# A decode kernel of two interleaved layers: the load of ScalarE's function table first on its engine, and new orders of the same tasks on four engines

## The chip, the cores and the metric

The kernel runs on one core of a Trainium2 chip. The core has five instruction streams that run side by side and meet through semaphores: TensorE (PE in the profile, its weight loads PEld), VectorE (DVE), ScalarE (ACT), GpSimd (POOL) and SyncE (SP), which here does nothing but issue transfers. Each engine works through its instructions strictly in the order in which they are written; an instruction whose semaphore has not come yet holds up everything behind it on that engine. The metric is the device time of one launch in microseconds (us), as the median of several runs. Times inside the kernel come from the profile of one further execution.

## What is computed

Eight batches, each with one row of D = 448 numbers, go through an attention layer (A) and an MLP layer (B), and then through both once more with the same weights and the same K and V caches:

```python
def _A_ref(x, k_cache, v_cache, wq, wo):          # Hq = 16, Hkv = 8, Dh = 256
    W = min(4096, max(256, Sk // 4))              # Sk = 4096, W = 1024
    q = (x @ wq)                                  # 448 x 4096, 16 heads of 256
    k = jnp.repeat(k_cache[:, :, Sk - W:, :], 2, axis=1)
    v = jnp.repeat(v_cache[:, :, Sk - W:, :], 2, axis=1)
    p = _softmax(einsum("bhqd,bhkd->bhqk", q, k) * Dh ** -0.5)
    return einsum("bhqk,bhkd->bhqd", p, v) @ wo   # 4096 x 448

def _B_ref(x, w1, w2):                            # F = 1792
    return _silu(x @ w1) @ w2

x = A_x
x = x + _A_ref(_layernorm(x), ...)
x = x + _B_ref(_layernorm(x), ...)
x = x + _A_ref(_layernorm(x), ...)
x = x + _B_ref(_layernorm(x), ...)
```

All is bf16. Only the last W = 1024 positions of each cache are read: per batch eight K heads and eight V heads of 1024 x 256, 512 KB each.

## The kernel before

**Data.** One K or V head fills one of R = 30 slots in SBUF, `slots`, 128 partitions by 2048 numbers. `load_kv` (L453, its DMA at L456) loads them in the sequence batch 0 K0 to K7, V0 to V7, batch 1 K0 to K7 and so on; a slot is loaded again once its last reader is done. wq, wo, w1 and w2 are loaded once: wq ahead of the first K, wo and w2 behind batch 0's K7, w1 behind its V7. The last two slots, 28 and 29, serve as scratch space at the start (x, the squares, the first q, the row sums of wo and w2, and the place into which ACT writes what it only wants to sum); the loads that take them over wait for those uses. Both layers read a head out of the same slot, so the second attention of a batch must run while its K and V are still there.

**Stages.** Each batch b runs through these, named by the strings that the code gives to its tasks:

- *start*, once for all batches (`start_rows`, L569): constants are cleared on DVE (L330 to L377, bank clears at L350 and L352 of the eight PSUM banks among them); x is turned into columns on PE ("xT", into bank 7), masked on DVE ("xb0", L576), its statistics are made ("sq8" on ACT, L547; "sqh8", "st8" on DVE; "stat8" on PE), it is centred ("x0", DVE), multiplied by wq for all batches at once ("q1", L591), and brought into the form that the scores need ("q1r", "q1T", "q1sel", and "q1s", one half copied by DVE, the other by ACT).
- *row sums* (`row_sums`, L426), once: the mean of each row of wo and w2 is written beside it, so that the layer norm's mean comes out of the same product. Groups of rows take turns between DVE ("rsum2", "rsum3", L435; the copy "rsumd", L438) and ACT ("rsum", L443, twenty of them; the copy "rsumd", L447).
- *layer 1 attention*: POOL spreads q over the key heads in two halves ("qbd1", L622); DVE transposes each K slot in two halves ("KT0" to "KT7", L632); PE makes the scores in eight blocks, four for K0 to K3 and four for K4 to K7 ("S0.0", "S0.1", L648); softmax (L657): DVE maximum and its spreading ("max0" L665 to "mb0" L669), ACT exp (L672), PE permutation ("perm0", L674), DVE transposition ("turn0", L676), sums of the rows (L680) and their reciprocals. Then the values in two parts ("PVA" L729 for V0 to V3, "PVD" L748 for V4 to V7); each part is copied out by ACT ("oevA.0", "oevA.1" L715; "oevD" L723), turned by PE ("oTA", "oTD", L702) and scaled by DVE ("oTevA", "oTevD", L696). The output projection runs in two halves ("woA", "woD", L801) and is copied out by ACT ("rowb1", L1091).
- *chain* (L856): residual and layer norm ("xinit", "fold1", the x column "xb1" L827, "stat1" L834, ACT's variance "var1" L837, POOL's power "pow1" L839), the MLP ("w1" L518, its turn "yT" L538, "tanh" L846, "hT" L847, "w2" L865, "rowb2" L869), the next residual and norm ("fold2", "xb2", "x2b", "stat2", "var2", "pow2"), and q of layer 2 in two halves ("wq0", "wq1" L892; "qT" L538, "qm" L901, "qd" L905, and ACT's copy "qbd2" L909).
- *layer 2 attention* of the same batch ("S1.0", "S1.1", "max1", "exp1", ..., values "PV1.0", "PV1.1", L729, "oev1" L723), interleaved with layer 1 of the next batch.
- *tail*: batches 0 to 6 are taken together through layer 2's output projection and MLP beside batch 7's chain (`final_rows`, L912: "wo8", "w18", "tanh8" L978, "h8" L979, "w28" L983, "rowb9" L991); batch 7 ends by itself (`final_last`, L997).

PE also gets short fillers: `busy` (L850) puts in products with zeros ("zero", L853, 48 of them) whose results nobody reads.

**What sets the order.** The code above does not fix the order in which an engine runs its tasks. `Plan.add` (L56) only records each task with the tiles that it reads and writes. `schedule` (L91) then lays out each of the four computing engines by a string in `ORDER` (L16 to L35): every character is a base-62 digit, the place of the next task among those of this engine that are left, in program order ("0" is the first one left; "." announces two digits). PE has 509 tasks, DVE 421, ACT 167, POOL 38. SP is not in the table: its loads stay in program order. `emit` (L108) then works out which semaphores each task must wait for, so that the same data flows whatever the order; ACT issues its three transfers ahead of its tasks.

The load of ACT's function table is one such task:

```python
act(lambda e: e.preload_act_table_set("exp_and_others"), [], [], -1, "init")     # L328
```

It reads and writes no tile, so nothing waits for it and it may stand anywhere on ACT. In the order of before it is ACT's 73rd task, behind the exp of batch 3.

Of the kernel before, what the change touches and what calls it, by code (L numbers as in the profile page):

```python
# [14 lines left out]

ORDER = {  # L16
    "pe": (
        "0000000q11111111133311c11312221130000033001700510330011117777000400444433200011610440333022021000220"
        "1777101000111117777000030444433200011615551002201101000220006051000111111777700040044443320001166151"
        "4002201120103300006605100011111777700040044442220001161551400220110100330000605103001111177770004004"  # L20
        "4443220001161551400220110100333990010000011111177770004004444232000111551400220111010002200066055100"
        "cccc0000006000044444320001107066605504401220000c22aaa22801050002014403355550222333355553322523432201"
        "000111000"),
    "dve": (
        "2AB1liliiv4vousks2uquCuxAoO15xxJxd8s5vIpsBt4ooxb6clojllftvjfcnmm82g9f0h8d3e6bdc9a3435114402110082302"
        "54202210098880870705ab0abc0088700555550000000a08980870705aa09a09097700555550000000098880870605ab09a0"
        "b097700555550000000a08989078005ab09a0b087700555550000100a08889078005aa09a0b097700555550000000a089890"
        "77060baa09c0087700555550000100a089807770d0b5aa0ab9901005555500001100acia0g90e8a098706004440300100022"
        "011333312122211110000"),
    "act": (  # L30
        "12222233232222322c22a3333632221111111113312112111111111331211111111111130201000000000000220100000000"
        "0000220110000000000022010000000000030201110100000403300001111101010"),
    "pool": (
        "00000011001102200301032002200201001000"),
}  # L35


# [1123 lines left out]
```

## Time and profile before

| | |
|---|---|
| time, median of 3 runs | 233.13 us (232.94, 233.13, 233.14) |
| time of the profiled execution | 235.56 us |
| its span, first to last instruction | 233.7 us |
| mean granted clock of TensorE | 0.963 |
| busy: PE | 170.5 us, 73% of the span, 3616 matmuls |
| busy: PE's weight loads | 93.5 us, 40% (beside the matmuls) |
| busy: DVE | 158.4 us, 68%, 421 instructions |
| busy: ACT | 68.2 us, 29%, 203 instructions |
| busy: POOL | 22.8 us, 10%, 42 instructions |
| moved by DMA | 78.20 MB |

How to read what follows. A row of the timeline has the time of its start from the start of the span, its length, its engine, its line in the kernel, the operation, output and input tiles with their shape, how many instructions it sums up, and in brackets the idle time of the engine just before it with what ended it. The chain of waits is the sequence of work that ended last, followed back from the last instruction. A row of the windows gives, for one stretch of time, the busy time of each engine and its number of instructions. The granted clock is the share of full speed that TensorE was given. Tiles are named by their allocation: a name such as slot or w_sb stands for all buffers of that name, and qbd holds, beside q, the exponentials and the probabilities.

### The profile page before, as it was taken

To read this page: it belongs to the slowest core of one execution; us is meant where nothing else is said; L and a number is where in the kernel's file an instruction comes from. 1 tells how busy PE (TensorE), PEld (TensorE's weight loads), DVE (VectorE), ACT (ScalarE), POOL (GpSimd) and SP (SyncE) were. 2 spreads that over 40 slices of the span, in tenths; PEclk is the share of its full clock that TensorE was granted. 3 is DMA by queue.
4 is the path that set the end of the run, shared out by engine and by line. 5 is a ranking of instruction groups with operands and counts; after the bars stand their busy time and mean duration, and the time that the engine had idled before them with its cause. 6 is when DMAs were issued, how large, how long until landed. Compare 5 with 4: busy or idle time off the path is not lost.

```text
span 233.7 us, 8172 instructions
## 1 busy us (share of the span) xinstructions
PE 170.5 (73%) x3616; PEld 93.5 (40%) x3616; DVE 158.4 (68%) x421; ACT 68.2 (29%) x203; POOL 22.8 (10%) x42
## 2 busy tenths in 40 slices
PE   0000562368879887988898898879797978899985
PEld 0000530123444454445444443544363335556453
DVE  6029998967874995588488649947675597355642
ACT  2000003995223323321532233233213322143321
POOL 1000220001200200200021011002000110010200
PEclk9999999559999999999999999999799999999999
DMA  6999999999999999999999999999999999500000
GB/s 165 411 407 409 380 380 396 412 407 410 403 405 405 407 409 364 410 408 405 391 407 409 360 365 416 408 403 407 407 365 263 414 407 363 191 3 3 3 4 4
DMA packets 23401, 78.20 MB, mean 335 GB/s; under 512 B 3127, under 2 KB 6086, under 8 KB 22982
## 3 DMA queue, kind: packets, MB, share of 16 engines
q1 hardware_dynamic: 22806, 77.30, 85.2%
q8 instruction: 28, 0.46, 0.8%
q10 hardware_dynamic: 560, 0.38, 0.7%
q14 instruction: 7, 0.06, 0.1%
HBM read 77.67 MB, written 0.01 MB: 332 GB/s over the span
## 4 chain that ended last, share of the span: by engine, by line
PE 43%; SPq 21%; DMA 14%; DVE 10%; ACT 6%; issue 4%; POOL 1%; DVEq 0%; ACTq 0%
DMA slot<-in_A_k_cache_dram 14%; SPq L456 12%; PE bank L648 10%; PE bank L729 6%; SPq L413 6%; DVE slot L632 4%; PE bank L892 3%; PE bank L801 3%; PE bank L518 3%; PE bank L865 2%; PE bank L748 2%; PE bank L853 2%; PE bank L905 2%; PE bank L702 2%; PE bank L674 1%
## 5 line engine op out<-in xcount | busy, mean ns | idle before, releaser
L632 DVE STREAM_TRANSPOSE slot<-slot 128x512 uint32<-128x512 uint32 x128 | 82.7, 686 | 19.2 <-DMA slot<-in_A_k_cache_dram 19.0
L648 PE MATMUL bank<-slot,qbd 128*16 128x256 bf16 (+1 forms) x1024 | 40.8, 287 | 6.8 <-ACT qbd L909 3.3
L729 PE MATMUL bank<-slot,qbd 128*4 128x512 bf16 (+1 forms) x384 | 28.6, 388 | 7.2 <-DVE w_sb L438 6.2
L648 PEld LDWEIGHTS bank<-slot,qbd 128*16 128x16 bf16 (+1 forms) x1024 | 23.2, 88 | 18.2 <-ACT qbd L909 6.5
L839 POOL TENSOR_TENSOR fcols<-fcols 128x1 f32<-128x1 f32 x17 | 9.4, 554 | 117.8 <-ACT fcols L837 107.5
L672 ACT ACTIVATE qbd<-bank,mm 128x256 bf16<-128x256 f32 x17 | 8.0, 472 | 36.9 <-DVE mm L669 36.9
L676 DVE STREAM_TRANSPOSE qbd<-bank 128x256 bf16<-128x256 bf16 x17 | 8.1, 478 | 15.0 <-PE bank L674 15.0
L892 PE MATMUL bank<-wq_sb,xbz 128*2 128x256 bf16 x512 | 17.2, 275 | 0.1
L853 PE MATMUL bank<-ident,cols 128*128 128x512 bf16 x48 | 16.7, 403 | 0.0
L622 POOL TENSOR_TENSOR qbd<-q1s,fcols 128x256 bf16<-128x256 bf16 x16 | 9.6, 614 | 63.5 <-PE bank L702 58.1
L801 PE MATMUL bank<-wo_sb,q1s 128*1 128x449 bf16 x252 | 15.5, 368 | 0.1
L729 PEld LDWEIGHTS bank<-slot,qbd 128*4 128x4 bf16 (+1 forms) x384 | 7.9, 84 | 17.9 <-DVE w_sb L438 6.4
L909 ACT ACTIVATE qbd<-bank 128x256 bf16<-128x256 f32 x16 | 6.1, 383 | 30.1 <-PE bank L905 30.1
L715 ACT ACTIVATE qbd<-bank 128x256 bf16<-128x256 f32 x20 | 7.7, 383 | 18.6 <-PE bank L729 16.2
L892 PEld LDWEIGHTS bank<-wq_sb,xbz 128*2 128x2 bf16 x512 | 11.3, 82 | 3.8 <-DVE xbz L827 1.7
L538 DVE STREAM_TRANSPOSE bank<-bank 128x256 f32<-128x256 f32 (+1 forms) x25 | 10.8, 436 | 2.9 <-PE bank L518 1.7
L748 PE MATMUL bank<-slot,qbd 128*12 128x512 bf16 (+3 forms) x124 | 11.2, 410 | 1.3 <-ACT qbd L715 1.3
L723 ACT ACTIVATE qbd<-bank 128x512 bf16<-128x512 f32 x14 | 8.3, 594 | 12.5 <-PE bank L748 10.3
L865 PE MATMUL bank<-w_sb,q1s 128*1 128x449 bf16 x98 | 7.2, 382 | 5.5 <-DVE q1s L847 5.5
L665 DVE TENSOR_REDUCE mm<-bank 128x1 f32<-128x256 f32 x17 | 7.2, 421 | 5.6 <-PE bank L648 5.1
L696 DVE TENSOR_TENSOR q1s<-bank,q1s 128x16 bf16<-128x16 f32 (+1 forms) x18 | 3.0, 167 | 10.3 <-PE bank L702 9.8
L551 PE MATMUL bank<-xb,cols 128*128 128x8 bf16 x4 | 0.3, 172 | 13.1 <-DVE slot L549 13.1
(164 smaller groups left out, 231.4 us busy)
## 6 DMA issues: line engine op xcount, KB each, us to landing
slot<-in_A_k_cache_dram SPq DMA_DIRECT2D x64, 512.0 KB, 8.6
slot<-in_A_v_cache_dram SPq DMA_DIRECT2D x64, 512.0 KB, 11.1
wo_sb<-in_A_wo_dram SPq DMA_DIRECT2D x1, 3584.0 KB, 25.7
wq_sb<-in_A_wq_dram SPq DMA_DIRECT2D x3, 1024.0 KB, 8.6
w_sb<-in_B_w_dram SPq DMA_DIRECT2D x1, 1568.0 KB, 28.1
w_sb<-in_B_w_dram SPq DMA_DIRECT2D x1, 1344.0 KB, 17.5
wq_sb<-in_A_wq_dram SPq DMA_DIRECT2D x1, 256.0 KB, 3.5
wq_sb<-in_A_wq_dram ACTq DMA_DIRECT2D x1, 256.0 KB, 4.0
```

The costliest lines, as they stand in the source:

```text
L413: dma(lambda e: e.dma_start(w2_sb[:].rearrange("p (g n) -> p g n", n=PW)[:, :, R0:M1], B_w2.rearrange("(g p s) n -> p g (s n)", p=P, s=2)) ...
L456: dma(lambda e: e.dma_start(slots[s][:, :].rearrange("p (u d) -> p u d", d=DH), cache[b, kvh, S0:SK, :].rearrange("(p u) d -> p u d", p=P) ...
L538: dve(lambda e: e.transpose(view(bank[bi][:], n, [(2, n // 32), (n // 16, 16), (1, 2)]), bank[bi][:, 0:n].rearrange("p (g r s) -> p g r s" ...
L622: pool(lambda e, k2=k2: e.tensor_tensor(qdata(0, k2), q1s[:, b, 64 * k2:64 * k2 + 64].rearrange("p (n r) -> p n r", r=2).unsqueeze(3) .bro ...
L632: dve(lambda e, v=v: e.transpose(v, v), SL(s, h), SL(s, h), b, "KT%d" % k)
L648: fns.append(lambda e, w=w, j=j, kv=kv, cb=cb, par=par: e.matmul(sc[32 * j:32 * j + up_to, 0:256], w, kv, start=(cb == 0 and par == 0), st ...
L729: return [lambda e, u=u: e.matmul(bank[OB[L] if ob is None else ob][32 * j:32 * j + 2 * n, :], pT_sb[L if qi is None else qi][:, pcol(u, c ...
L748: pe([lambda e, t=t, c0=c0, w=w, kvh=kvh: e.matmul(bank[OB[0]][32 * t:32 * t + 2 * w, :], pT_sb[0][:, pcol(2 * t, c0):pcol(2 * t, c0) + 2 ...
L801: fns.append(lambda e, i=i, w=w, c0=c0: e.matmul(bank[XB][32 * (i % 4):32 * (i % 4) + 1, c0:c0 + D + 1], oT(i), w, start=(i < 4), stop=(i ...
L853: pe(lambda e: e.matmul(bank[SC[1]][:, :], cols[:, 3:4].broadcast_to([P, P]), view(ident[:], 0, [(0, 4), (1, P)]), start=True, stop=True), ...
L865: fns.append(lambda e, f=f, w=w, c0=c0: e.matmul(bank[XB][32 * (f % 4):32 * (f % 4) + 1, c0:c0 + D + 1], hTr[b][:, f:f + 1], w, start=(f < 4),
L892: pe([lambda e, j=j, c=c, s=s, wb=wb, k2=k2: e.matmul(bank[wb][32 * j:32 * j + 2, 0:256], pair(b, xcol(c, k2), s), view(wq_sb[:], c * HD + ...
```

## The change

Only the four strings of `ORDER` change. The tasks, what each reads and writes, the loads, and SP's order are the same; so are all sizes.

```diff
 ORDER = {
     "pe": (
-        "0000000q11111111133311c11312221130000033001700510330011117777000400444433200011610440333022021000220"
-        "1777101000111117777000030444433200011615551002201101000220006051000111111777700040044443320001166151"
...
+        "00v00000111111111333121b1333310410005500390277222010111117777000002444420210901105003330201100003300"
+        "1700500300111117777000030444442200011615551002201100003302006055000201111777700003044444220001115144"
...
     "dve": (
-        "2AB1liliiv4vousks2uquCuxAoO15xxJxd8s5vIpsBt4ooxb6clojllftvjfcnmm82g9f0h8d3e6bdc9a3435114402110082302"
...
+        "qGoQIji1z.161kwIv.111iuttEx3kBSBBPra95Exxx80qgxlIC6rpppxfkcmvh4cbis1qp25i6ha2gce51abam424f7402444847"
...
     "act": (
-        "12222233232222322c22a3333632221111111113312112111111111331211111111111130201000000000000220100000000"
-        "0000220110000000000022010000000000030201110100000403300001111101010"),
+        "00222231233334f4413b44422252220110000000201100000000000022011000000000002201100000000000220110000000"
+        "0000220110000000000022011000000000030201110100000403300001100001010"),
     "pool": (
-        "00000011001102200301032002200201001000"),
+        "00010301001000100200020000100201001000"),
 }
```

Read back into tasks, the strings say this:

- **ACT.** The table load is the first task. At the start, before ran sq8, exp0 of batch 0, and then the row sums; after, five row sums stand between sq8 and that exp. Two of ACT's copies of row sums come later: w2's first behind oevA.0, w2's second behind var1 of batch 0. In the last batch rowb9 comes ahead of the evacuation oevL0.0; smaller swaps between neighbouring batches are left out here.
- **DVE.** At the start, before clears five banks and some constants first, masks x at place 22 and transposes the first K half (slot 0) at place 27. After, three banks (6, 1, 0) and six small constants come first, the 10th task is the first half of slot 1, the clear of bank 7 is the 12th, the mask of x again the 22nd; K0 is transposed 69th and 71st. Of the sixteen K halves of batch 0 fifteen stand ahead of q's "q1T" and all ahead of "q1s", where before ten and eleven did; rsum3 and one rsum2 stand ahead of max0 of batch 0. In the later batches oTevD comes ahead of the next batch's KT0, four K halves stand between it and xb1, and in batches 3 to 5 three halves instead of two between xb1 and yT. In the last batch h8 comes behind the second maximum.
- **PE.** The first filler stands ahead of q1; in batch 0 the second q1sel is earlier, woA stands behind oTD, and no filler is left between fold1, stat1 and w1. The four blocks of S1.1 stand three ahead of perm0 and one behind it in most turns (all four ahead in batch 0, one in batch 5), where they were two and two in most. From batch 3 on woA stands behind oTD, and one PV1.1 ahead of oTD. stat2 stands ahead of wq0 in batches 0 to 5, where before it did so in batch 5 alone. Fillers move: batch 4 has none between w1 and w2 (before, batch 5 had none there). In the last batch the first of the two permutations and xinitL stand ahead of w28.
- **POOL.** The two halves of qbd1 of batch 0 change places; pow1 and pow2 stand ahead of the second qbd1 half in several batches.

More of the change, by code (lines that the diff above doesn't have):

```diff
@@ L17 @@
     "pe": (
-        "0000000q11111111133311c11312221130000033001700510330011117777000400444433200011610440333022021000220"
-        "1777101000111117777000030444433200011615551002201101000220006051000111111777700040044443320001166151"
-        "4002201120103300006605100011111777700040044442220001161551400220110100330000605103001111177770004004"
-        "4443220001161551400220110100333990010000011111177770004004444232000111551400220111010002200066055100"
-        "cccc0000006000044444320001107066605504401220000c22aaa22801050002014403355550222333355553322523432201"
@@ L23 @@
-        "000111000"),
-    "dve": (
-        "2AB1liliiv4vousks2uquCuxAoO15xxJxd8s5vIpsBt4ooxb6clojllftvjfcnmm82g9f0h8d3e6bdc9a3435114402110082302"
[L26 to L29, printed above, removed]
+        "00v00000111111111333121b1333310410005500390277222010111117777000002444420210901105003330201100003300"
@@ new lines @@
+        "1700500300111117777000030444442200011615551002201100003302006055000201111777700003044444220001115144"
+        "4410011101103300177166111101111777700003044444320001161144441001110110022280166111101111177770000304"
+        "4443320001161144441001110100330017771111101111177770050004444422000116114444100111011033a09207710100"
+        "cccc000000600004444322100110706660550440122000022bbb22980105000201440335555j302233335555332242232015"
+        "100011100"),
+    "dve": (
+        "qGoQIji1z.161kwIv.111iuttEx3kBSBBPra95Exxx80qgxlIC6rpppxfkcmvh4cbis1qp25i6ha2gce51abam424f7402444847"
+        "5663344413bb0aa11981816c0a0a9a0088700555504000000098980870605bb0aba0077700555550000000088880870605bb"
+        "0a9a0077700555550000000098880877060bba0ba0077700555550000000098880877005bb0a9a0087700555550000000098"
+        "880778060bba099007770055555000000090888807870b0aac099990100555550000110b0cib09g90d080777050444030200"
+        "0022224033311122211110000"),
```

## The prediction

> **What bounds the kernel now.** I read the page first, then the windows, the chain of work that ended last, and the timeline. From the page: the span, the granted clock in 40 slices of 5.84 us, and the K transposes on DVE (count, then busy and mean ns, then idle before).
>
> ```profile
> span 233.7 us, 8172 instructions
> PEclk9999999559999999999999999999799999999999
> L632 DVE STREAM_TRANSPOSE slot<-slot 128x512 uint32<-128x512 uint32 x128 | 82.7, 686 | 19.2 <-DMA slot<-in_A_k_cache_dram 19.0
> ```
>
> From the windows (stretch, its length, then busy us of PE, PEld, DVE, ACT, POOL, the granted clock, DMA share and GB/s):
>
> ```profile
> 0.00:15.30 15.30, 0.36 (x5) 0.28 (x5) 4.02 (x26) 1.51 (x2) 0.70 (x6) 1.00 0.88 316
> 15.30:36.05 20.75, 8.85 (x221) 6.36 (x221) 18.00 (x61) 0.00 (x0) 2.85 (x3) 1.00 1.04 391
> ...
> 160.00:170.00 10.00, 8.45 (x141) 3.96 (x129) 7.26 (x17) 2.75 (x8) 1.74 (x3) 0.83 1.03 408
> ```
>
> The DMA engines stream at about 400 GB/s all through: at 408 a 512 KB slot (524,288 bytes) takes 1.28 us. Transposing a K slot takes two DVE instructions of 82.7/128 = 0.65 us. Now the chain (start, length, what):
>
> ```profile
> 47.50 15.63 DMA slot<-in_A_k_cache_dram
> ...
> 67.55 0.44 DVE mm L665
> ...
> 88.85 0.44 DVE mm L665
> ...
> 152.81 0.44 DVE mm L665
> ...
> 179.29 9.99 DMA slot<-in_A_k_cache_dram
> ...
> 195.07 1.08 PE bank L648 x32
> ```
>
> And one row of the timeline, the first maximum of batch 6:
>
> ```profile
> 175.57 0.42 DVE L665 TENSOR_REDUCE mm<-bank 128x1 f32<-128x256 f32 x1 [0.57 <-PE bank L648]
> ```
>
> Up to 63 us the chain is loading. Then each batch takes one turn from its first softmax maximum (L665) to the next: 88.85 - 67.55 = 21.30 us, and (152.81 - 67.55)/4 = 21.32 on average. Sixteen slots want 16 x 1.28 = 20.5 us of DMA, less than a turn, so the turn is bound by the handshakes of PE, ACT, DVE and POOL. The turn up to 175.57 took 22.76: its granted clock is the 0.83 above. At the end the last K loads come back into the chain (179.29), and from 195 us the last batch runs out on PE.
>
> **The change, part by part.** *The table load.* From ACT's timeline:
>
> ```profile
> 2.57 1.28 ACT L547 ACT_TABLE_LOAD   x1 [2.57 <-issue]
> 5.26 0.23 ACT L547 ACTIVATE slot<-xb 128x32 f32<-128x32 bf16 x1 [1.40 <-DVE xb L576]
> ...
> 111.89 1.28 ACT L328 ACT_TABLE_LOAD   x1
> ...
> 113.96 0.38 ACT L715 ACTIVATE qbd<-bank 128x256 bf16<-128x256 f32 x1 [0.79 <-PE bank L729]
> ```
>
> Before has two loads. One stands at 2.57, put before the first activation because L328's own is far down the order; it is behind ACT's three DMA issues and ends at 3.85. L328's own is at 111.89, in batch 3. With L328 first I expect one load, again behind those DMA issues and over long before ACT is needed. The one at 111.89 ends at 113.17 and its engine then waits 0.79 us more for PE, so taking it away gives 0.0 (bounds 0 and, if its cover were gone, -1.28). The Trainium skill ("ScalarE: Activation LUTs", What ACT_TABLE_LOAD costs) speaks of about 2.66 us for a switch, a drain included. By that ACT would have been held until about 114.5, past the 113.96 at which it started: this trace shows 1.28 and no drain. A load into the set already active may differ; I leave it as a rival.
>
> *The start.* Rows of the timeline, in order of time:
>
> ```profile
> 1.25 2.65 DVE L331 MEMSET bank<- 128x512 f32 x5
> 15.32 0.71 DVE L632 STREAM_TRANSPOSE slot<-slot 128x512 uint32<-128x512 uint32 x1 [9.58 <-DMA slot<-in_A_k_cache_dram]
> 36.05 0.42 DVE L665 TENSOR_REDUCE mm<-bank 128x1 f32<-128x256 f32 x1 [0.71 <-PE bank L648]
> 37.23 2.91 DVE L435 TENSOR_REDUCE slot<-wo_sb 128x6 f32<-128x2688 bf16 x1
> 37.41 0.47 ACT L672 ACTIVATE qbd<-bank,mm 128x256 bf16<-128x256 f32 x1 [31.92 <-DVE mm L669]
> 39.24 0.58 ACT L443 ACTIVATE slot<-w_sb 128x448 bf16<-128x448 bf16 x1 [1.27 <-DMA w_sb<-in_B_w_dram]
> 39.94 0.58 ACT L443 ACTIVATE slot<-w_sb 128x448 bf16<-128x448 bf16 x1
> 40.06 3.93 DVE L435 TENSOR_REDUCE slot<-w_sb 128x4 f32<-128x1792 bf16 x2
> 53.91 0.22 ACT L447 ACTIVATE wo_sb<-slot 128x6 bf16<-128x6 f32 x1
> 54.22 2.58 DVE L632 STREAM_TRANSPOSE slot<-slot 128x512 uint32<-128x512 uint32 x4 [0.62 <-DMA slot<-in_A_k_cache_dram]
> 54.28 0.93 PE L801 MATMUL bank<-wo_sb,q1s 128*1 128x449 bf16 x16
> 55.27 0.55 ACT L1091 ACTIVATE rowb<-bank 128x450 bf16<-128x450 f32 x1 [0.47 <-PE bank L801]
> 63.16 0.71 DVE L632 STREAM_TRANSPOSE slot<-slot 128x512 uint32<-128x512 uint32 x1 [0.41 <-DMA slot<-in_A_k_cache_dram]
> 63.80 0.42 DVE L538 STREAM_TRANSPOSE bank<-bank 128x256 f32<-128x256 f32 x1
> 65.47 2.04 PE L648 MATMUL bank<-slot,qbd 128*16 128x256 bf16 x64 [0.47 <-ACT qbd L909]
> ```
>
> Before, DVE clears its constants first (4.02 us of work), then stands 9.58 us at slot 0 of K. After, the tenth DVE task is the transpose of slot 1, which lands one slot later: 15.3 + 1.3 = 16.6. Behind it stand the clear of bank 7, on which PE's first transposition of x waits, and so the whole path to q; and most of the clears. What stands ahead of it is three bank clears (3 x 0.53) and six small ones, about 2.1 us. So from 16.6 DVE has to do what before did in 20.75 us, plus 4.0 - 2.1 = 1.9 of clears, less about 1.2 that are left for later, plus two row sums that now stand ahead of the first maximum (2.91 and 3.93/2 = 1.97): 16.6 + 20.75 + 0.7 + 4.9 = 42.9, against 36.05. All sixteen K transposes now stand ahead of that maximum and of q's copy but for one half, where before ran five of them under POOL's spreading of q. POOL now spreads the second half of q first, and PE's first filler stands ahead of q's product; both fall beside those row sums and cost nothing while DVE is last.
>
> Then ACT. It runs five row sums from 39.24 (0.70 each, 39.94 - 39.24) to 42.7 and stands until the first exp: 42.9 + (37.41 - 36.05) = 44.3, over at about 45.0. Before, all twenty sums with their copies took 54.13 - 39.24 = 14.9 without a pause; without five sums (3.5) and a copy (0.1) 11.3 are left, so wo's last sums are ready at about 56.3, not 54.13 (53.91 + 0.22): +2.1. The output projection, its evacuation at 55.27 and DVE's next K transposes (behind the second head evacuation in the new order, so at about 55.5 to 56, not 54.22) move by as much. In both orders thirteen half transposes stand between there and q's turn; before took 63.80 - 54.22 = 9.6 us for them, 0.41 of it the wait at 63.16. From 55.75 that gives 65.3, and about 0.6 for the first x column, which comes late by more than DVE does: 65.9. **Start: +2.1 us.** The lower bound is +0.8: the new order takes q's turn ahead of the last slot, one landing (1.28) earlier. The upper bound is +4.0: the stretch is at half clock in before (the two 5s of PEclk), and the two halves of wo (0.93 each) may take twice as long.
>
> SP's queue: the loads that take over the two scratch slots wait for ACT's last sums, which now end after the first variance, near 59. The one behind them waits for layer 2's scores at about 67.6 + 1.0 = 68.6 (half of 2.04). Loads are queued until 47.50 + 15.63 + 6 x 1.28 = 70.8, so DMA may run short there, by about 1 us; that is inside the bounds.
>
> *The turns of batches 1 to 6.* From the chain, in batch 2:
>
> ```profile
> 104.53 1.06 PE bank L892 x32
> 106.15 0.56 POOL fcols L839
> 107.15 0.40 PE bank L905 x4
> ```
>
> In before, statistics come behind wq's first half on PE, so POOL's power ends (106.71) after the second half could. Most new turns issue the statistics first: 1.06 earlier for POOL. But then the two halves themselves bind: 104.53 + 2 x 1.06 = 106.65, against 107.15, and in most turns one more block of scores (x8 of 64 in 2.04: 0.26) now stands ahead of the statistics. Gain per turn: 0 to 0.5, I take 0.15. In batches 3 to 6 one value block moves behind the output projection, into ACT's evacuation: up to 0.2. Against that DVE holds its K transposes back until the last head evacuation, and has four halves (2.6 us) between it and the x column, and three instead of two (0.65 more) ahead of the MLP's turn in batches 3 and 4: 0.1 to 0.4 lost. In batch 1 all four score blocks of layer 2 now stand ahead of the permutation and the other maximum ahead of the turn (0.44), about 0.5 lost. POOL's power ahead of the second spreading, and the moved fillers, cost nothing where PE waits anyway. **Turns: +0.3 in all**, bounds -2.4 (0.4 in each of six) and +2.0.
>
> *The last batch.* From the timeline:
>
> ```profile
> 219.36 0.22 DVE L979 SCALAR_TENSOR_TENSOR slot<-slot 128x98 bf16<-128x98 f32 x1
> 219.64 0.92 PE L983 MATMUL bank<-w_sb,slot 128*7 128x448 bf16 x14
> 221.38 0.36 PE L683 MATMUL bank<-qbd,cols 128*128 128x8 bf16 x8 [0.56 <-DVE qbd L676]
> ```
>
> L979 leaves the path to the first exp (up to 0.2 gained) and L983 goes between the first permutation and L683, into a wait of 0.56 that it overruns by 0.92 - 0.56 = 0.4 at most. ACT's copy of L983's result ahead of an evacuation, the earlier x columns and two fillers fewer lie beside PE work. **+0.1**, bounds -0.2 and +0.4.
>
> *What the end gives back.* From the timeline of batch 6:
>
> ```profile
> 185.46 1.31 DVE L632 STREAM_TRANSPOSE slot<-slot 128x512 uint32<-128x512 uint32 x2 [1.26 <-DMA slot<-in_A_k_cache_dram]
> ```
>
> The last K loads are waited for. If compute is 2.4 later there and the loads are later by less, part of that wait goes. **-0.7**, bounds -1.3 and 0.
>
> *The sum.* The profiled execution took 235.56 (span 233.7, 1.86 around it), 2.43 more than the median of the runs, 233.13. I carry this distance over: 235.56 + 2.1 + 0.3 + 0.1 - 0.7 = 237.4 under the profiler, **234.9 us** as median.
>
> **The rivals.** *Faster: the turns pay.* If POOL's power is what each turn waits for last and the scores moved ahead of the statistics fit under the x column's wait, each of six turns gives 0.4, which with the start at its lower bound is 233.13 + 0.8 - 2.4 = 231.5. For it: 106.15 follows directly on wq in the chain. Against: 106.65 and the DVE queue. It decides from 0.35 a turn, where it outweighs the 2.1 of the start. *No change: loads cover the start.* If batch 0 is bound by the landing of K1 anyway (47.50 + 15.63 = 63.1), DVE's lateness up to 1.6 us is hidden and the rest is repaid: 233.1 to 233.6. Against: DVE is behind those loads in my sum, not ahead. *Slower still: half clock.* Between 160 and 170 the granted clock fell to 0.83, in the turn of batch 5, where the order has no filler between w1 and w2; that turn cost 22.76 - 21.32 = 1.4. After, batch 5 has two fillers there and batch 4 none: 234.9 + 1.4 = 236.3 if the timed runs of before lack such a stretch and after has one. The Trainium skill ("TensorE: Matmul & The Clock Gate", What's actually happening) says that activity in free-running windows of about 3.4 us decides the rate; so a stretch may come and go between runs. No run here shows that yet. *The table load counts after all*, or a second one stays where it was: 234.9 - 1.3 = 233.6 if its 1.28 was on the path.
>
> **How the numbers follow.** Forecast 0.50 (its own range 233.7 to 235.9), faster turns 0.22, covered start 0.13, half clock 0.12, table load 0.03. A measurement of this kernel tells apart about 0.2%, 0.47 us. So faster 0.23, same 0.15, slower 0.62. The range leaves out about half of the faster case and the top of the half-clock case: 231.6 to 236.4.
>
> **What would show it.** One table load, near 2.6, and ACT's exp of batch 3 followed by nothing. DVE's first transpose at about 16.6 with some 12 us of idle time before it; the first L665 near 43, not 36; the first L672 near 44, not 37.4; L1091 near 58, not 55.27; the first 64-block L648 after it near 67.6, not 65.47. Distances between the L672 of later batches near 21.3; under 20.9 would make the prediction wrong, and so would a first L1091 at 55 to 56.

## The result, and the profile after

The changed kernel takes 235.16 us (median of 20 runs, 234.41 to 238.82) against 234.31 us of the kernel before in runs beside it (20 runs, 232.76 to 237.80). The ratio is 1.0055 with a 95% interval of 1.0034 to 1.0076: slower by about 1.3 us (0.8 to 1.8). The forecast was 234.9 from a base of 233.13, a ratio of 1.0076. Ratios here leave out runs more than 1.5% above the fastest of their kernel: one of these 20 and three of the 20 before, and in the fastest version below four of twelve in its first measurement (e6) and one of twelve in its second (e12), so that its lead is less sure than its interval looks.

The two profiled executions alone would have told the opposite: 235.56 us before, 234.99 us after. The page of the changed kernel, the rows that answer to those shown of before:

```profile
span 233.2 us, 8180 instructions
...
PEclk9999999956999999999999999999999999999999
...
L632 DVE STREAM_TRANSPOSE slot<-slot 128x512 uint32<-128x512 uint32 x128 | 81.9, 684 | 14.0 <-DMA slot<-in_A_k_cache_dram 13.9
```

The second dip of PEclk is gone: before had a stretch at half clock in the turn of batch 5, and that turn took 22.76 us instead of 21.3. Some executions of this order have such a stretch and others don't: in the first experiment the kernel before with nothing but the table load moved has none, and its span is 231.5 us. All comparisons by stage below are therefore made with that execution, called the reference execution. The first K slot lands at 15.3 to 16.6 us after the start of the span, differently in each execution, and shifts the start that follows, so the table gives that landing too. Counting from it doesn't take out all chance: two executions of one and the same kernel (e6 and e12 below) then still differ by 0.9 us at the first maximum of batch 1.

| us | first K slot landed | first maximum (L665) | first exp (L672) | first L1091 | first maximum of batch 1 | of batch 7 | span |
|---|---|---|---|---|---|---|---|
| before | 15.29 | 36.05 | 37.41 | 55.27 | 67.55 | 196.19 | 233.7 |
| reference execution | 15.64 | 36.40 | 37.75 | 55.51 | 68.03 | 194.18 | 231.5 |
| after | 15.31 | 43.30 | 44.45 | 57.65 | 69.15 | 196.07 | 233.2 |

So, counted from that landing, the first maximum is 7.2 us late, L1091 2.5, and batch 1's maximum 1.45 (69.15 - 15.31 against 68.03 - 15.64). From there six turns take 126.92 us against 126.15, and the last batch 37.1 against 37.3. Most of the loss stands at the start. From the timeline of the changed kernel, in order of time (start, length, engine, line, what, idle before):

```profile
2.57 1.28 ACT L328 ACT_TABLE_LOAD   x1 [2.57 <-issue]
...
16.62 0.71 DVE L632 STREAM_TRANSPOSE slot<-slot 128x512 uint32<-128x512 uint32 x1 [13.54 <-DMA slot<-in_A_k_cache_dram]
...
37.58 0.69 DVE L610 CAST q1s<-bank 128x512 bf16<-128x512 f32 x1 [0.18 <-PE bank L602]
38.19 2.94 DVE L435 TENSOR_REDUCE slot<-wo_sb 128x6 f32<-128x2688 bf16 x1
38.35 1.18 POOL L622 TENSOR_TENSOR qbd<-q1s,fcols 128x256 bf16<-128x256 bf16 x2 [12.70 <-DVE q1s L610]
...
39.59 3.59 PE L648 MATMUL bank<-slot,qbd 128*16 128x256 bf16 x64 [2.04 <-POOL qbd L622]
...
41.40 1.98 DVE L435 TENSOR_REDUCE slot<-w_sb 128x4 f32<-128x1792 bf16 x1
42.07 0.58 ACT L443 ACTIVATE slot<-w_sb 128x448 bf16<-128x448 bf16 x1
43.30 0.41 DVE L665 TENSOR_REDUCE mm<-bank 128x1 f32<-128x256 f32 x1
44.45 0.47 ACT L672 ACTIVATE qbd<-bank,mm 128x256 bf16<-128x256 f32 x1 [1.71 <-DVE mm L669]
...
56.05 0.22 ACT L447 ACTIVATE wo_sb<-slot 128x6 bf16<-128x6 f32 x1
...
57.65 0.55 ACT L1091 ACTIVATE rowb<-bank 128x450 bf16<-128x450 f32 x1 [0.92 <-PE bank L801]
```

DVE stands until 16.62. q's copy L610 comes at 37.58; behind it POOL spreads q, PE makes its scores from 39.59 to 43.18, and only then is there a maximum to take. ACT's five sums are over at 42.65 and it waits 1.71 us for the exp. Its last sums are ready at 56.27.

The chain of work that ended last shows what that does. First the changed kernel (start, length, what), then the reference execution:

```profile
44.45 0.56 ACT qbd L672 x2
...
48.40 0.67 ACT slot L443 x2
...
54.28 0.49 ACT qbd L723
...
55.08 2.55 PE bank L801 x29
...
57.65 0.55 ACT rowb L1091
```

```profile
47.51 16.06 DMA slot<-in_A_k_cache_dram
...
68.03 0.44 DVE mm L665
```

Before, the start was bound by loads: the chain goes through batch 1's K slots until 63.57. After, it goes through exp, ACT's sums and the output projection. The engines have overtaken the loads as the bound, by 1 to 2 us in these two executions.

### The profile page after: what moved, and what is told of

The parts are those of the page before. It is cut to its first block, busy times and chain, and to the rows that moved or that the text cites. A ratio compares the mean times of both kernels' runs of the same rounds, so it can differ in the third digit from the quotient of the medians.

```text
span 233.2 us, 8180 instructions
## 1 busy us (share of the span) xinstructions
PE 168.1 (72%) x3616; PEld 93.8 (40%) x3616; DVE 157.7 (68%) x421; ACT 66.5 (29%) x202; POOL 22.8 (10%) x42
## 4 chain that ended last, share of the span: by engine, by line
PE 55%; DVE 17%; ACT 11%; DMA 9%; issue 6%; SPq 1%; ACTq 0%; DVEq 0%
PE bank L648 12%; DMA slot<-in_A_k_cache_dram 9%; PE bank L729 8%; DVE slot L632 6%; PE bank L892 6%; PE bank L801 5%; ACT slot L443 4%; PE bank L518 3%; PE bank L748 3%; PE bank L865 2%; PE bank L905 2%; PE bank L702 2%; ACT qbd L909 2%; PE bank L834 1%; PE bank L674 1%
## 5 line engine op out<-in xcount | busy, mean ns | idle before, releaser
L648 PE MATMUL bank<-slot,qbd 128*16 128x256 bf16 (+1 forms) x1024 | 40.2, 285 | 6.9 <-ACT qbd L909 3.6
L729 PE MATMUL bank<-slot,qbd 128*4 128x512 bf16 (+1 forms) x384 | 27.0, 381 | 2.5 <-DVE qbd L676 2.5
L892 PE MATMUL bank<-wq_sb,xbz 128*2 128x256 bf16 x512 | 16.3, 275 | 0.1
L801 PE MATMUL bank<-wo_sb,q1s 128*1 128x449 bf16 x252 | 14.8, 371 | 0.0
L729 PEld LDWEIGHTS bank<-slot,qbd 128*4 128x4 bf16 (+1 forms) x384 | 8.4, 84 | 13.3 <-DVE qbd L676 3.0
L696 DVE TENSOR_TENSOR q1s<-bank,q1s 128x16 bf16<-128x16 f32 (+1 forms) x18 | 3.1, 174 | 13.7 <-PE bank L702 12.8
L748 PE MATMUL bank<-slot,qbd 128*12 128x512 bf16 (+3 forms) x124 | 10.3, 411 | 2.0 <-ACT qbd L715 2.0
L665 DVE TENSOR_REDUCE mm<-bank 128x1 f32<-128x256 f32 x17 | 7.0, 415 | 6.0 <-PE bank L648 6.0
L672 ACT ACTIVATE qbd<-bank,mm 128x256 bf16<-128x256 f32 x17 | 8.0, 471 | 7.8 <-DVE mm L669 7.8
L865 PE MATMUL bank<-w_sb,q1s 128*1 128x449 bf16 x98 | 6.5, 353 | 4.6 <-DVE q1s L847 4.5
```

The costliest lines, as they stand in the source:

```text
L648: fns.append(lambda e, w=w, j=j, kv=kv, cb=cb, par=par: e.matmul(sc[32 * j:32 * j + up_to, 0:256], w, kv, start=(cb == 0 and par == 0), st ...
L729: return [lambda e, u=u: e.matmul(bank[OB[L] if ob is None else ob][32 * j:32 * j + 2 * n, :], pT_sb[L if qi is None else qi][:, pcol(u, c ...
L748: pe([lambda e, t=t, c0=c0, w=w, kvh=kvh: e.matmul(bank[OB[0]][32 * t:32 * t + 2 * w, :], pT_sb[0][:, pcol(2 * t, c0):pcol(2 * t, c0) + 2 ...
L801: fns.append(lambda e, i=i, w=w, c0=c0: e.matmul(bank[XB][32 * (i % 4):32 * (i % 4) + 1, c0:c0 + D + 1], oT(i), w, start=(i < 4), stop=(i ...
L865: fns.append(lambda e, f=f, w=w, c0=c0: e.matmul(bank[XB][32 * (f % 4):32 * (f % 4) + 1, c0:c0 + D + 1], hTr[b][:, f:f + 1], w, start=(f < 4),
L892: pe([lambda e, j=j, c=c, s=s, wb=wb, k2=k2: e.matmul(bank[wb][32 * j:32 * j + 2, 0:256], pair(b, xcol(c, k2), s), view(wq_sb[:], c * HD + ...
```

## The experiments

Only the strings of the orders are edited. All times are compared with runs of the kernel before on the same chip.

| | kernel | ratio to before | 95% interval |
|---|---|---|---|
| e1 | before, table load first | 0.9997 | 0.9967 to 1.0026 |
| e2 | before, new start | 1.0072 | 1.0041 to 1.0103 |
| e3 | after, old start | 0.9981 | 0.9952 to 1.0011 |
| e4 | before, ACT's new start alone | 1.0008 | 0.9976 to 1.0040 |
| e5 | after, K1 later on DVE | 1.0016 | 0.9988 to 1.0044 |
| e6 | after, DVE's old order up to mb0 | 0.9967 | 0.9940 to 0.9994 |
| e7 | before, DVE's new start alone | 1.0239 | 1.0203 to 1.0275 |
| e8 | before, stat2 ahead of wq0 | 1.0091 | 1.0058 to 1.0124 |
| e9 | after, two DVE sums behind max0 | 1.0288 | 1.0238 to 1.0338 |
| e10 | e9, five K halves behind q | 1.0240 | 1.0194 to 1.0285 |
| e11 | after, DVE's old order up to hT | 1.0017 | 0.9981 to 1.0053 |
| e12 | e6 again | 0.9963 | 0.9932 to 0.9993 |

The same stages as above, for the runs that the text uses:

| us | first K slot landed | first maximum | first exp | first L1091 | first maximum of batch 1 | of batch 7 | span |
|---|---|---|---|---|---|---|---|
| e2 | 15.88 | 43.86 | 45.01 | 58.52 | 70.34 | 196.32 | 233.6 |
| e3 | 15.92 | 36.69 | 38.04 | 56.17 | 68.10 | 194.31 | 231.5 |
| e4 | 16.01 | 36.77 | 43.32 | 56.81 | 68.36 | 194.34 | 231.8 |
| e5 | 16.11 | 42.60 | 43.75 | 57.21 | 68.68 | 195.25 | 232.2 |
| e6 | 16.24 | 37.32 | 42.98 | 55.91 | 67.54 | 193.53 | 230.5 |
| e7 | 16.24 | 44.21 | 45.35 | 61.75 | 73.30 | 200.50 | 238.0 |
| e9 | 15.98 | 43.87 | 45.09 | 62.50 | 75.48 | 201.84 | 238.8 |
| e10 | 16.05 | 42.94 | 44.16 | 61.58 | 73.98 | 200.27 | 237.3 |
| e11 | 16.11 | 37.20 | 43.19 | 56.58 | 68.11 | 195.76 | 233.0 |
| e12 | 15.99 | 37.07 | 43.64 | 56.58 | 68.19 | 194.13 | 231.1 |

### Which part carries the loss (e1 to e3)

e1 moves the one task on ACT:

```diff
     "act": (
-        "12222233232222322c22a3333632221111111113312112111111111331211111111111130201000000000000220100000000"
+        "001111122121111211b119222252111000000000220100100000000022010000000000002201000000000000220100000000"
```

> The kernel before with one edit: the load of ScalarE's table is ACT's first task. If its place is worth nothing (my reading): one table load, at about 2.6 us, none in batch 3, the first L665 still at about 36.05 and the time within 0.4 us of before. If the load in batch 3 was on the path: 1.28 us faster.

0.9997: no difference, and the profile has one load, L328's at 2.57. The 1.28 us in batch 3 were free.

e2 takes the new order on all engines up to the end of batch 0's MLP and keeps the old one from there; e3 is its complement. The first lines that differ, of PE, e2 and then e3 against before:

```diff
-        "0000000q11111111133311c11312221130000033001700510330011117777000400444433200011610440333022021000220"
+        "00v00000111111111333121b1333310410005500300700510330011117777000400444433200011610440333022021000220"
...
-        "0000000q11111111133311c11312221130000033001700510330011117777000400444433200011610440333022021000220"
+        "0000000q11111111133311c11312221130000033001716611110111117777000002444420210901105003330201100003300"
```

> The kernel before with the new order up to the end of batch 0's MLP on all four engines (PE to w2, DVE to hT, ACT to rowb2, POOL to pow1), the old order from there. If the start carries the loss: first L665 near 43.3, first L1091 near 57.7, max0 of batch 1 about 1.6 us later than in before, and the time 0.8 to 1.6 us above before. If the loads cover the start and the later orders carry the loss: the same first L665, but the time within 0.4 us of before.

> The complement: the old order up to the end of batch 0's MLP, the new order from there on. If the start carries the loss: first L665 near 36.05, turns of about 21.4 us, and the time between 0.4 us faster and 0.4 us slower than before. If the later orders carry it: 1.0 to 1.5 us slower than before, as in the changed kernel.

e2 is slower by 1.7 us (1.0 to 2.4, with 234.1 us as 1), e3 perhaps faster by 0.4 (between 1.1 faster and 0.3 slower); together 1.3, as measured for the whole change. The start carries all of it. In e2 the first maximum of batch 1 comes 2.07 us later than in the reference execution, counted from the first K slot; in the whole change 1.45. The 0.6 between them is less than the 0.9 by which e6 and e12 differ, so it doesn't show that the new orders behind the start take anything back.

### Which engine (e4, e6, e7)

e4 and e7 are the kernel before with the new start on one engine alone. ACT's string of e4, and the head of DVE's in e7:

```diff
-        "12222233232222322c22a3333632221111111113312112111111111331211111111111130201000000000000220100000000"
+        "00222231233334f4413b44422252220110000000220100100000000022010000000000002201000000000000220100000000"
...
-        "2AB1liliiv4vousks2uquCuxAoO15xxJxd8s5vIpsBt4ooxb6clojllftvjfcnmm82g9f0h8d3e6bdc9a3435114402110082302"
+        "qGoQIji1z.161kwIv.111iuttEx3kBSBBPra95Exxx80qgxlIC6rpppxfkcmvh4cbis1qp25i6ha2gce51abam424f7402444847"
```

> The kernel before with only ACT's new order up to rowb2 of batch 0 (five row sums ahead of the first exp, the rest of ACT, DVE, PE and POOL as before). If the lateness of the new start comes from DVE: ACT's sums end where exp and sums together end, 39.24 + 14.9 + 0.7 = 54.8 instead of 54.13, first L1091 near 56 and the time 0 to 0.8 us above before. If it is ACT's five sums ahead of the exp that make the start late: first L672 near 42.8, L1091 near 57.7 and the time 0.8 to 1.6 us above before.

> The kernel before with only DVE's new order up to hT of batch 0; ACT keeps its old order, with the first exp ahead of all its sums. If ACT's sums set the end of the start: first L672 near 44.4, the sums run from 45.0 for 14.9 us, first L1091 near 61 and the time 2.5 to 5 us above before, so that ACT's new order is what keeps the loss small. If the sums are covered by the loads: L1091 late, but the time 1.3 to 1.8 us above before, as with the whole new start.

ACT alone: the exp moves from 37.75 to 43.32, L1091 from 55.51 to 56.81 (0.9 once the landing of the first K slot is taken off), and nothing is left of that at batch 1's maximum, since the K loads cover it: 1.0008. DVE alone: 5.6 us slower, rather more than expected. With the exp ahead of all twenty sums, sums that could run from 39 us on stand behind an exp that comes at 45.35, and L1091 slips to 61.75. So DVE's order is the whole loss, and the new start on the other engines, with ACT's five sums ahead of the exp, takes back about 3.9 of its 5.6 us (1.0239 against 1.0072 in e2).

e6 is the changed kernel with DVE's old order up to mb0 of batch 0, its first 95 tasks. The head of its string against after:

```diff
-        "qGoQIji1z.161kwIv.111iuttEx3kBSBBPra95Exxx80qgxlIC6rpppxfkcmvh4cbis1qp25i6ha2gce51abam424f7402444847"
+        "2AB1liliiv4vousks2uquCuxAoO15xxJxd8s5vIpsBt4ooxb6clojllftvjfcnmm82g9f0h8d3e6bdc9a3435114402110084403"
```

> The changed kernel with DVE's old order up to the spreading of the first maximum (mb0 of batch 0) and all else new. If DVE's lateness there is the cause of the whole loss: first L665 near 36.1 to 36.8, first L672 near 42.8, first L1091 near 56.1, max0 of batch 1 near 68.2, and the time between 0.8 us faster and 0.4 us slower than before, as with the old start on all engines. If the K transposes of batch 1, held back until the second head evacuation in the rest of the new DVE order, carry it: the same first L672, but max0 of batch 1 near 69 and the time 1 us or more above before.

0.9967: the loss is gone, and by this ratio the kernel is faster than before by 0.8 us (0.1 to 1.4); over all twelve runs its mean is 0.2 us above that of before. e12 measured it again.

> The same kernel as the changed one with DVE's old order up to mb0 of batch 0, a second time, to see whether it is faster than before: 0.3 to 1.3 us below before if the first measurement holds, within 0.3 us of it if that was chance.

0.9963; over all twelve runs the mean is 0.4 us below that of before. The chain of e12 goes through the loads again until 55 us:

```profile
36.81 18.30 DMA slot<-in_A_k_cache_dram
...
55.13 2.58 DVE slot L632 x4
```

### What in DVE's order (e5, e9, e10)

e5 moves the two halves of K1 from places 10 and 16 to behind the first sqh8:

```diff
-        "qGoQIji1z.161kwIv.111iuttEx3kBSBBPra95Exxx80qgxlIC6rpppxfkcmvh4cbis1qp25i6ha2gce51abam424f7402444847"
+        "qGoQIji1z1kwIv1iuttEx3kBRRSBBPra95Exxx80qgxlIC6rpppxfkcmvh4cbis1qp25i6ha2gce51abam424f74024448475663"
```

> The changed kernel with one edit: the two halves of K1 on DVE move from places 10 and 16 to behind the first sqh8 (place 26), so that the clears and the mask of x no longer stand behind slot 1's landing. If DVE's wait for slot 1 makes the start late: first L665 near 40.8 (43.3 less the 2.5 us of other work between 16.6 and 20.6), first L672 near 42.8 (now held by ACT's five sums, over at 42.7), first L1091 near 56.1, and the time 0.5 to 1.2 us below the changed kernel, that is between 0.1 us faster and 0.8 us slower than before. If the wait is covered by something else: first L665 near 43.3 and the time as in the changed kernel, 1.3 us above before.

The time came as expected (1.0016, 0.9 us below the changed kernel, though the two intervals overlap), the size of the step did not: counted from the first K slot the first maximum is 1.5 us earlier, not 2.5, and batch 1's 1.3. The first exp, in e5 and then in e6, shows what reaches the time:

```profile
43.75 0.47 ACT L672 ACTIVATE qbd<-bank,mm 128x256 bf16<-128x256 f32 x1 [0.15 <-DVE mm L669]
```

```profile
42.98 0.46 ACT L672 ACTIVATE qbd<-bank,mm 128x256 bf16<-128x256 f32 x1
```

In the changed kernel ACT stood 1.71 us between its five sums and this exp, and its last sums were ready at 56.27, against 54.78 in e6. In e5 ACT stands 0.15 us, in e6 not at all. So with ACT's new order a later maximum costs about what ACT waits for it behind the five sums. The wait of one DVE instruction for one load, with the clears and x behind it, is thus the largest part of the loss.

e9 moves the two row sums of DVE behind the maximum (one behind mb0, one behind turn0):

```diff
-        "qGoQIji1z.161kwIv.111iuttEx3kBSBBPra95Exxx80qgxlIC6rpppxfkcmvh4cbis1qp25i6ha2gce51abam424f7402444847"
+        "qGoQIji1z.161kwIv.111iuttEx3kBSBBPra95Exxx80qgxlIC6rpppxfkcmvh4cbis1qp25i6ha2gce51aba4247402444c4777"
```

> The changed kernel with one edit on DVE: its two row sums ahead of max0 of batch 0 go behind it (rsum3 behind mb0, rsum2 and its copy behind turn0). If the two sums make the first maximum late, as the sum in the prediction had it (4.9 us of the way to 42.9): first L665 near 38.4, first L672 near 42.8 and the time below the changed kernel. If they lie beside POOL's spreading and PE's scores, as the trace of the changed kernel suggests (its scores end at 43.2): first L665 stays near 43.3, and since a sum of 2.9 us now stands ahead of turn0, first L1091 comes at 58 to 59 and the time is 0 to 1.5 us above the changed kernel.

From the timeline of e9:

```profile
43.87 0.42 DVE L665 TENSOR_REDUCE mm<-bank 128x1 f32<-128x256 f32 x1 [4.54 <-PE bank L648]
...
44.91 2.91 DVE L435 TENSOR_REDUCE slot<-wo_sb 128x6 f32<-128x2688 bf16 x1
47.74 0.46 DVE L676 STREAM_TRANSPOSE qbd<-bank 128x256 bf16<-128x256 bf16 x1
...
58.80 0.17 DVE L696 TENSOR_TENSOR q1s<-bank,q1s 128x16 bf16<-128x16 f32 x1
...
62.50 0.55 ACT L1091 ACTIVATE rowb<-bank 128x450 bf16<-128x450 f32 x1 [3.90 <-PE bank L801]
```

The maximum is where it was; in place of the sums DVE stands 4.54 us and waits for PE's scores. So the two sums cost nothing where the change put them: they fill a wait. Behind the maximum they stand between exp and the head evacuations, the first of which (L696) comes at 58.80 instead of 54.33, and the kernel is 5.5 us slower than the changed one, far more than expected.

e10 adds to e9 that the last five K halves go behind q's copy:

```diff
-        "qGoQIji1z.161kwIv.111iuttEx3kBSBBPra95Exxx80qgxlIC6rpppxfkcmvh4cbis1qp25i6ha2gce51aba4247402444c4777"
+        "qGoQIji1z.161kwIv.111iuttEx3kBSBBPra95Exxx80qgxlIC6rpppxfkcmvh4cbis1qp256a2c51aaaabaa4247402444c4777"
```

> The kernel of the run before this one, and the last five K halves of batch 0 (both of K0, one of K4, K3 and K5) behind q1s instead of ahead of q1r, q1T and q1s. If it is q's own path on DVE (K transposes ahead of q) that makes the first maximum late: q's copy L610 near 35, first L665 near 40.3, first L672 near 42.8 (ACT's five sums), and the time 0.5 to 1.2 us below the changed kernel. If the wait for slot 1 alone is the cause: first L665 stays above 42.5 and the time as in the changed kernel or above.

From the timeline of e10:

```profile
39.29 3.59 PE L648 MATMUL bank<-slot,qbd 128*16 128x256 bf16 x64 [3.18 <-DVE slot L632]
...
42.94 0.42 DVE L665 TENSOR_REDUCE mm<-bank 128x1 f32<-128x256 f32 x1 [2.67 <-PE bank L648]
```

By its numbers this falls on the second reading (42.94 is above 42.5, and the time is above that of the changed kernel), but neither number decides: counted from the first K slot the maximum lies between the two, and the time has e9's edit in it. q's copy comes 2.2 us earlier (36.15 - 16.05 against 37.58 - 15.31), but PE's scores now wait for the K halves instead of POOL, and the first maximum gains 1.1 us only, of the 7.2 by which it is late; e5 gave 1.5. What makes the maximum late is thus not one item but DVE's whole row: the first K half 1.3 us later, the clears behind it, and 3.59 us of scores that begin only after the last K half, where before they ran from 32.17 on, beside the last halves.

### The turns, and an open question (e8, e11)

e8 sets stat2 ahead of wq0 in six batches of the kernel before, one character in each:

```diff
-        "0000000q11111111133311c11312221130000033001700510330011117777000400444433200011610440333022021000220"
+        "0000000q11111111133311c11312221130000033001700500330011117777000400444433200011610440333022021000220"
```

> The kernel before with one edit in PE's order: stat2 moves ahead of wq0 in batches 0 to 4 and 6 (in batch 5 it stands there already). POOL's second power comes about 1.06 us earlier in these turns. If a turn waits for it: from max0 to max0 20.9 us or less and the time 1 to 2.4 us below before. If wq's two halves bind behind it (my reading): turns of 21.3 us as before, and the time within 0.5 us of before.

Neither held: 2.1 us slower (1.4 to 2.9). From the timelines of batch 2, the reference execution and then e8:

```profile
104.99 1.08 PE L892 MATMUL bank<-wq_sb,xbz 128*2 128x256 bf16 x32
106.01 0.25 PE L834 MATMUL bank<-xbz 128*128 128x1 bf16 x4
106.19 1.08 PE L892 MATMUL bank<-wq_sb,xbz 128*2 128x256 bf16 x32
107.64 0.40 PE L905 MATMUL bank<-qm,spread 128*128 128x64 bf16 x4 [0.36 <-DVE qm L901]
```

```profile
106.16 0.24 PE L834 MATMUL bank<-xbz 128*128 128x1 bf16 x4 [0.34 <-ACT q1s L887]
106.32 1.99 PE L892 MATMUL bank<-wq_sb,xbz 128*2 128x256 bf16 x64
...
108.72 0.40 PE L905 MATMUL bank<-qm,spread 128*128 128x64 bf16 x4 [0.41 <-DVE qm L901]
```

stat2 writes into the bank out of which ACT copies x (L887), and so must wait for that copy; wq's first half, which writes another bank, used to run in this wait. In e8 PE stands 0.34 us instead, both halves run later (x's copy to L905: 2.89 us, against 2.61), and POOL's earlier power is of no use. The first four turns take 21.6 to 21.7 us, against 21.3 in most turns of the reference execution. In the changed kernel scores stand in that place, and its turns are near 21.4. Four times 0.3 is 1.2 of the 2.1 us; e8's profiled execution also has a stretch at half clock in batch 5, and how much of the rest that is isn't settled.

e11 was to ask whether the new order of batch 1's K transposes is what makes e6 faster than before. Its string against that of e6:

```diff
-        "2AB1liliiv4vousks2uquCuxAoO15xxJxd8s5vIpsBt4ooxb6clojllftvjfcnmm82g9f0h8d3e6bdc9a3435114402110084403"
-        "12201111999900870705ba0a9a0088700555504000000098980870605bb0aba0077700555550000000088880870605bb0a9a"
+        "2AB1liliiv4vousks2uquCuxAoO15xxJxd8s5vIpsBt4ooxb6clojllftvjfcnmm82g9f0h8d3e6bdc9a3435114402110082302"
+        "54202210098880870705ba0a9a0088700555504000000098980870605bb0aba0077700555550000000088880870605bb0a9a"
```

> The changed kernel with DVE's old order up to hT of batch 0, so that against the run with the old order up to mb0 only the K transposes of batch 1 come earlier again (ahead of the second head evacuation, and all of them but three ahead of q's turns). If that new order of the K transposes is what made the run with the old order up to mb0 0.3% faster than before: the time here is 0.3 to 0.8 us above that run, near before, and max0 of batch 1 comes 0.5 to 1 us later. If it is PE's, ACT's or POOL's orders: the same time and the same max0 of batch 1 as in that run.

The question was put wrongly: read back into tasks, both orders have batch 1's K halves in the same sequence, behind the second head evacuation, and differ in fourteen places only, all of them row sums, their copies and what stands between: e11 has one sum more ahead of turn0 and the copies later. So this run says nothing of the K transposes. The ratio, 1.0017, is 0.5% above e6 and e12, but its interval overlaps theirs; over all twelve runs its mean lies 0.3 us above that of before, e6's 0.2 above. Batch 1's maximum, counted from the first K slot, came at 52.00 against 51.30 in e6 and 52.20 in e12. In the profiled execution of e11 the loss stands in batch 3, where DVE waited 1.13 us for a K slot. What would make e6 and e12 faster than before therefore stays open: the later orders (e3, 0.9981) may give half of it, and five sums ahead of the exp, with DVE in time, the other; no run separates these. That the loss of the change is gone is shown by both ratios and by batch 1's first maximum (51.30 and 52.20 against 53.84 in the changed kernel). A lead over before is not shown: both ratios have one, of 0.1 to 1.6 us, but over all their runs e6 lies 0.2 us behind and e12 0.4 ahead.

## Why the prediction came out, step by step

The forecast was a slowdown of 1.8 us; measured are about 1.3 (0.8 to 1.8). The direction and the place, DVE's order at the start, were right. That the total is so near is in part luck: one step has the wrong work in it and still the right length, and another takes off 0.7 us for a gain that does not come.

- **The table load: 0.** Right (e1). One load, at 2.57 us, behind ACT's issues, as forecast.
- **The start: +2.1.** The size is about right: 1.45 us at batch 1's first maximum in the changed kernel and 2.07 in e2's trace, 1.7 (1.0 to 2.4) in e2's time. The stations came: first transpose 16.62 (16.6), first maximum 43.30 (42.9), exp 44.45 (44.3), last sums 56.27 (56.3), L1091 57.65 (near 58); only the scores of batch 1 began earlier than forecast, at 66.70 (67.6). But one step of the working was wrong, and its error was hidden by luck. The sum counted the two row sums, 4.9 us, as DVE work on the way to the maximum, and said that POOL's spreading and PE's fillers fell beside them. It is the other way round: after q's copy, over at 38.27, POOL and the scores need 1.2 + 3.6 us, and the sums lie beside those (e9). Before, this leg stood beside five K halves; the change moved these ahead of q, and so the leg itself comes on top. The sum left the leg out and put the sums in its place; both are about 4.9 us long, and so the number came right. The leg in the kernel before, q's copy and the scores:

```profile
29.98 0.69 DVE L610 CAST q1s<-bank 128x512 bf16<-128x512 f32 x1
32.17 3.83 PE L648 MATMUL bank<-slot,qbd 128*16 128x256 bf16 x64 [1.80 <-POOL qbd L622]
```

- **The half clock as upper bound.** In the changed kernel the 32 products of the output projection run together behind oTD and take 2.58 us, against twice 0.93 in e6; L1091 waits for them and not for the last sums, which were ready at 56.27. The prediction had this only in its upper bound. In the reference execution the two halves take 1.71 and 0.93 us, but the first runs earlier, from 51.71.
- **The turns: +0.3.** Six turns take 126.92 us after, 126.15 in the reference execution, 126.21 in e3 and 125.98 in e2; with the same later orders as the changed kernel, e6 takes 125.99 and e11 127.65. So the 0.8 us here lie within what single executions differ by, and no gain or loss of the later orders is shown. The gain that was counted for the earlier statistics is, by itself, a loss (e8): the sum saw that wq's halves bind, but not that stat2, put first, must wait for x's copy.
- **The last batch: +0.1.** 37.1 us after, 37.3 in the reference execution: 0.2 gained, inside the bounds.
- **What the end gives back: -0.7.** Wrong: nothing comes back. The turn into batch 7 takes 19.68 us after and 19.35 in the reference execution. The 1.26 us of waiting that the step was built on came after the half-clock stretch of before's one execution. The reference execution has, in the same turn, only this wait for a load:

```profile
180.97 0.71 DVE L632 STREAM_TRANSPOSE slot<-slot 128x512 uint32<-128x512 uint32 x1 [0.61 <-DMA slot<-in_A_k_cache_dram]
```

- **The distance between profile and median, 2.43 us.** It was carried over from before to after as if it were the profiler's. It was that stretch and chance: the changed kernel's profiled execution, 234.99, lies beside its median.
- **The rivals.** Faster turns: refuted by e3 and e8. Loads that cover the start: half true; they cover the 0.9 us of e4, not the 2 us of e2. The half clock moving to batch 4: not seen, since PEclk has no dip behind the start. It was before that lost time by it in some of its runs: batch 5's turn takes 22.76 us with the stretch and 21.26 without (reference execution). In 13 of its 82 runs beside the experiments the mean granted clock was near 0.963, as in its profiled execution, with a median of 234.6 us, against 233.9 for the 30 runs near 0.97 and 233.5 for the 35 with 1.00; the other four, near 0.993 and with a median of 235.8, fit one such stretch and no recorded one at the start.

## What to carry to other kernels

In a hand-made order of tasks, look at the first instruction of each engine that waits for a load and ask what stands behind it: here clears that depended on nothing stood 13.5 us behind one K slot. DVE's new order, of which this was a part, cost 5.6 us alone, and moving this one slot back gave 0.9 of the 1.3 us. Long work that nobody waits for yet, such as the row sums, belongs into waits; the same two sums cost nothing ahead of the maximum and more than 5 us behind it, so an order must be judged by both places of a task. And one profiled execution is a sample: before its waits are priced, compare its span with the timed runs, or take a second one.

## What the runs showed of the hardware

The granted clock that the views give can be missing for the first 60 us, and then reads 1.00. The windows of e9 and of e10 from 50 to 57 us (length, busy us of PE, PEld, DVE, ACT, POOL, clock, DMA share, GB/s), and one row of each timeline:

```profile
50.00:57.00 7.00, 4.38 (x46) 1.50 (x45) 6.87 (x9) 6.08 (x22) 0.00 (x0) 0.50 1.02 407
```

```profile
53.49 1.89 PE L748 MATMUL bank<-slot,qbd 128*16 128x512 bf16 x16 [2.01 <-ACT qbd L715]
```

```profile
50.00:57.00 7.00, 3.46 (x38) 1.11 (x37) 6.91 (x7) 6.84 (x25) 0.00 (x0) 1.00 1.03 411
```

```profile
52.56 1.89 PE L748 MATMUL bank<-slot,qbd 128*16 128x512 bf16 x16 [2.01 <-ACT qbd L715]
```

The same sixteen products take 1.89 us in both, at a shown clock of 0.50 and of 1.00. The trace of e10 has no clock event before 61.6 us, that of e9 none before 44.5, and the views take such a stretch as 1.00. And the first 64 products of the scores take 3.59 us in the changed kernel, where its window from 39.6 to 43.2 has 1.00 and its trace no clock event; 64 such products take 2.03 us at 109.85. So a mean clock of 1.000 does not show that PE ran at full speed at the start, and durations of like products decide. The Trainium skill ("TensorE: Matmul & The Clock Gate", Seeing it yourself) warns that such events in a trace are unreliable; these two executions agree.
